# Output products of the second PSUM bank declared independent of the copy that reads the first bank

## Chip, cores and metric

The kernel runs on one core of one Trainium2 chip. The metric is the device time of one execution in microseconds (us). Ratios are the mean time of one kernel's fast runs over the mean of the other's of the same rounds, so they are not quite the ratio of the medians that are quoted. The experiments ran on two chips; each had the kernel before in its rounds but not the changed kernel, so the ratios compare them best, and medians of different experiments should be compared only to about 1 us (those of the kernel before lie between 386.71 and 387.66). Engines: PE is TensorE, PEld its weight loads, DVE VectorE, ACT ScalarE, POOL GpSimd, SP the queue that issues most transfers.

## The reference

```python
w = softmax(weight, axis=-1)                      # 8 heads, 7 taps
x_pad = concat(zeros(B, 6, D), x)                 # B=8, S=4224, D=192
out = einsum('hk,bskhg->bshg', w, windows(x_pad)) # causal conv, one filter per head
proj = out @ w_in                                 # 192 -> 2*512
val, gate = proj[..., :512], proj[..., 512:]
h = a * h + val[:, t]                             # a = exp(A_log)[0], step by step; ys[t] = h
return (silu(gate) * ys) @ w_out                  # 512 -> 192
```

## The kernel before

Tokens are cut into blocks of 960, and the 512 inner channels into four groups of 128; a step is one block with one group. The loop does two steps in each repeat. PE makes value and gate products, each in a "full" part over 128 of the 192 input channels and a "half" part over the other 64; DVE scans the values, ACT takes SiLU of the gates, POOL multiplies. When 512 tokens are ready in all groups, an output unit multiplies them by `w_out`. In PSUM lie two value tiles and two "m" tiles of two banks each; the m tiles serve gates, conv products and output units in turn. ACT copies the conv result to SBUF (tile `yc`), and a DMA transpose turns it into `xc`, which the value and gate products of a later repeat read. Halo rows are the rows ahead of a sequence, which the convolution has to read as zeros.

```python
def out_mm(ps, u, k, cs):                  # bank k of the tile: 2 x 192 columns
    for c in cs:
        for j in range(k * UB // 2, (k + 1) * UB // 2):
            o = k * BANK + (j % 2) * D
            nc.tensor.matmul(ps[:, o : o + D], yr[c][:, ...], wout[:, c, :], ...)

def out_unit(u):
    ps = mtile()
    osb = o_pool.tile([P, UB, D], FP32, name="osb")
    for k in range(2):
        out_mm(ps, u, k, range(NC))        # eight products
        out_copy(nc.scalar, ps, osb, k)    # PSUM bank k -> SBUF, 128x384
    nc.sync.dma_start(o4[u], osb)
# ... in each repeat (s = 2 * p):
scan(s); val(s+1) full; gate(s) full; val(s+1) half; gate(s) half
val(s+2) half; gate(s+1) half; silu(s); mul(s); gate(s+1) full; val(s+2) full; silu(s+1)
scan(s+1); mul(s+1); [big input load]; out_unit(u); [zero halo rows]; conv_piece(...)
```

The framework places the waits. It takes the second eight products as writers of the tile that the first copy is still reading, and makes them wait, though they write another bank.

Of the kernel before, what the change touches and what calls it, by code (L numbers as in the profile page):

```python
# [36 lines left out]
def kernel(  # L37
# [9 lines left out]
    nc = tc.nc  # L47

    B, S, D = x.shape
# [4 lines left out]
    P = 128  # L54
    NC = DI // P
# [22 lines left out]
    of = out.rearrange("b s d -> (b s) d")  # L78
# [14 lines left out]
    def vtile():  # L93
        return ps_v.tile([P, 2 * BANK], FP32, name="pv")

    def mtile():
        return ps_m.tile([P, 2 * BANK], FP32, name="pm")

    def copy(eng, o, i):
        if eng is nc.scalar:  # L100
            eng.copy(o, i)  # L101
        else:
            eng.tensor_copy(o, i)

    def half(b):
        return SIZES[b] * M // 2
# [96 lines left out]
    for r in range(2):  # L203
# [4 lines left out]
        )  # L208
    xt0, _ = xtile(0)
    copy(nc.scalar, xt0[:, n0 : 2 * n0, :], xr[1])  # L210
    copy(nc.vector, xt0[:, 0:n0, :], xr[0])

    pt = mtile()
# [51 lines left out]
    def conv_evac(engs, ps, b, part):  # L265
        n = SIZES[b]
        nh = n // 2
        y = ytile(b)
        E = 2 * G
        pr = ps[0:M, :]  # L270
        W1 = P - 2 * E
        for eng, js in engs:
            j0, nj = js
            if part == 0:
                copy(
                    eng, view(y, j0 * E, [[E, nj], [P, n], [1, E]]),
                    view(pr, j0 * BANK, [[BANK, nj], [E, n], [1, E]]),
                )
            else:
                q = W1 // 2  # L280
                copy(
                    eng, view(y, 2 * E + j0 * q, [[q, nj], [P, n], [1, q]]),
                    view(pr, j0 * BANK, [[BANK, nj], [E, n], [1, q]]),
                )
                z = E - q
                for j in range(j0, j0 + nj):
                    copy(
                        eng,
                        view(y, n * P + j * z, [[P // 2, 2], [P, nh], [1, z]]),
                        view(pr, j * BANK + q, [[nh * E, 2], [E, nh], [1, z]]),  # L290
                    )
# [31 lines left out]
    wout = singles.tile([P, NC, D], BF16, name="wout")  # L323
# [10 lines left out]
    for part in range(2):  # L334
        ps = vtile()
# [64 lines left out]
    yr = [singles.tile([P, RING], BF16, name=f"y_{c}") for c in range(NC)]  # L400

    def ring(t, n):
        r = (t - SHIFT) % RING
        assert r + n <= RING
        return slice(r, r + n)
# [5 lines left out]

    def out_mm(ps, u, k, cs):
        r = ring(u * UT, UT)
        for c in cs:
            for j in range(k * UB // 2, (k + 1) * UB // 2):
                o = k * BANK + (j % 2) * D
                nc.tensor.matmul(  # L417
                    ps[:, o : o + D], yr[c][:, r.start + j * P : r.start + j * P + P],
                    wout[:, c, :], start=(c == 0 and j % 2 == 0), stop=(c == NC - 1),
                    skip_group_check=True,  # L420
                )

    def out_copy(eng, ps, osb, k):
        copy(
            eng, osb[:, k * UB // 2 : (k + 1) * UB // 2, :].rearrange("p b d -> p (b d)"),
            ps[:, k * BANK : k * BANK + 2 * D],
        )

    def out_unit(u):
        ps = mtile()  # L430
        osb = o_pool.tile([P, UB, D], FP32, name="osb")
        for k in range(2):
            out_mm(ps, u, k, range(NC))
            out_copy(nc.scalar, ps, osb, k)
        nc.sync.dma_start(o4[u], osb)

    def conv_piece(b, part):
# [14 lines left out]
    u = 0  # L452
    todo = [(b, part) for b in range(1, NSB) for part in range(2)]
    for p in range(NSTEP // 2):
# [32 lines left out]
        if u < NU - 1 and done_step(u) < s - late:  # L487
            out_unit(u)
            u += 1
# [10 lines left out]
    ps = mtile()  # L500
    for k in range(2):
        out_mm(ps, u, k, range(NC - 1))
    scan(s)
    mul(nc.vector, s)
    osb = o_pool.tile([P, UB, D], FP32, name="osb")
    for k in range(2):
        out_mm(ps, u, k, [NC - 1])
    for k in range(2):
        out_copy((nc.scalar, nc.vector)[k], ps, osb, k)
        h2 = slice(k * UB // 2, (k + 1) * UB // 2)  # L510
        (nc.scalar, nc.sync)[k].dma_start(o4[u, :, h2, :], osb[:, h2, :])
# [28 lines left out]
```

## Time and profile before

| | before |
|---|---|
| time, median | 387.66 us (387.17 to 388.15) |
| span of the profiled run | 385.9 us |
| PE / DVE / POOL / ACT busy | 86 / 80 / 78 / 70% |
| granted PE clock | 0.996 |

The busy shares alone name no culprit: four engines between 70 and 86%. The page's part 4, the chain that ended last by line, does:

```profile
PE pm L417 25%; PE pm L352 15%; PE pv L352 14%; PE pv L358 9%; ACT osb L101 8%; PE pm L248 7%; PE pm L358 7%; DVE h L392 2%; PE pm L187 2%; ACT sg L378 1%; POOL y L410 1%; DMA xc<-yc 1%; ACT yc L101 1%; ACT xb L130 0%; ACT xc L101 0%
```

The path is PE nearly throughout, with one foreign body: ACT's output copy (L101, tile `osb`) has 8% of the span. Since ACT is idle for 30% of the span, this entry points to an order that is enforced, not to a full engine.

### The profile page before, as it was taken

What the parts mean: (1) busy time and instruction counts of PE and PEld (TensorE: products, weight loads), DVE (VectorE), ACT (ScalarE), POOL (GpSimd) and SP (SyncE); (2) the same over time, 40 slices, a digit from 0 to 9 for tenths busy, and PEclk for the clock granted to TensorE, in tenths of its full rate; (3) what the DMA queues carried; (4) which work ended last, traced back from release to release, by engine and by line L of the source; (5) the groups of instructions that cost most, each with busy time, mean ns of one, the idle gap of its engine ahead of it and who ended that gap; (6) DMA issues with size and microseconds to landing.
All of it is one profiled execution on the core that took longest, in us unless ns stands there. A gap on an engine that the chain in (4) does not pass through costs nothing.

```text
span 385.9 us, 6702 instructions
## 1 busy us (share of the span) xinstructions
PE 330.5 (86%) x2555; PEld 194.6 (50%) x2555; DVE 310.2 (80%) x181; ACT 270.2 (70%) x437; POOL 302.7 (78%) x176
## 2 busy tenths in 40 slices
PE   8888888888998888888888888989888888988884
PEld 3444455544554555544555555545555555554553
DVE  3677888879887888878888888898888878888982
ACT  4487677776776777776777677777777777776662
POOL 5867987788778877788789777897789767778891
PEclk9899999999999999999999999999999999999999
DMA  9899999479945996489746994499449954444323
GB/s 186 93 136 132 133 178 208 120 127 189 184 120 122 138 206 155 121 118 177 169 109 123 185 202 121 121 161 219 120 106 153 203 131 111 109 111 112 98 88 125
DMA packets 124523, 55.16 MB, mean 143 GB/s; under 512 B 89622, under 2 KB 124298, under 8 KB 124490
## 3 DMA queue, kind: packets, MB, share of 16 engines
q1 hardware_dynamic: 84498, 39.20, 45.1%
q0 software_dynamic: 39248, 14.99, 34.4%
q10 hardware_dynamic: 744, 0.54, 0.5%
q8 instruction: 20, 0.33, 0.4%
q14 instruction: 13, 0.11, 0.1%
HBM read 31.45 MB, written 25.95 MB: 149 GB/s over the span
## 4 chain that ended last, share of the span: by engine, by line
PE 79%; ACT 11%; issue 4%; DVE 3%; POOL 1%; DMA 1%; DVEq 0%; ACTq 0%
PE pm L417 25%; PE pm L352 15%; PE pv L352 14%; PE pv L358 9%; ACT osb L101 8%; PE pm L248 7%; PE pm L358 7%; DVE h L392 2%; PE pm L187 2%; ACT sg L378 1%; POOL y L410 1%; DMA xc<-yc 1%; ACT yc L101 1%; ACT xb L130 0%; ACT xc L101 0%
## 5 line engine op out<-in xcount | busy, mean ns | idle before, releaser
L410 POOL TENSOR_TENSOR y<-sg,h 128x960 bf16<-128x960 bf16 (+2 forms) x143 | 278.2, 1967 | 71.4 <-ACT sg L378 71.3
L392 DVE TENSOR_TENSOR_SCAN h<-av,h,pv 128x960 bf16<-128x960 f32 (+4 forms) x132 | 261.6, 2018 | 55.8 <-issue 36.8
L378 ACT ACTIVATE sg<-pm 128x960 bf16<-128x960 f32 (+2 forms) x144 | 133.3, 952 | 36.0 <-PE pm L358 30.6
L417 PE MATMUL pm<-wout,y 128*128 128x192 bf16 x1056 | 108.2, 245 | 37.2 <-ACT osb L101 36.8
L417 PEld LDWEIGHTS <-y 128*128 128x128 bf16 x1056 | 89.8, 97 | 60.5 <-issue 47.4
L101 ACT COPY osb<-pm 128x384 f32<-128x384 f32 x131 | 62.6, 478 | 63.0 <-PE pm L417 60.8
L352 PE MATMUL pm<-xc,w 128*128 128x480 bf16 (+2 forms) x288 | 81.9, 366 | 1.1 <-ACT yc L101 0.7
L352 PE MATMUL pv<-xc,w 128*128 128x480 bf16 (+2 forms) x288 | 81.1, 362 | 1.5 <-DVE h L392 1.3
L352 PEld LDWEIGHTS <-w 128*128 128x128 bf16 x576 | 50.0, 98 | 61.6 <-issue 32.5
L101 ACT CAST yc<-pm 96x320 bf16<-96x320 f32 (+2 forms) x140 | 69.6, 552 | 5.1 <-PE pm L248 4.3
L358 PE MATMUL pv<-xc,w 64*128 64x480 bf16 (+2 forms) x288 | 53.1, 366 | 2.4 <-DVE h L392 2.4
L358 PE MATMUL pm<-xc,w 64*128 64x480 bf16 (+2 forms) x288 | 52.4, 361 | 0.0
L392 DVE TENSOR_TENSOR_SCAN h<-av,pv 128x768 bf16<-128x768 f32 (+4 forms) x32 | 45.6, 1434 | 5.2 <-issue 3.5
L358 PEld LDWEIGHTS <-w 64*128 64x128 bf16 x576 | 22.6, 94 | 47.4 <-issue 32.9
L248 PE MATMUL pm<-xb,tb 112*96 112x240 bf16 (+1 forms) x280 | 39.4, 263 | 5.6 <-ACT xb L130 5.3
L248 PEld LDWEIGHTS <-tb 112*96 112x96 bf16 x288 | 30.0, 123 | 8.3 <-issue 6.8
L124 POOL DMA_DIRECT2D xb<-in_x_dram x12 | 17.7, 1473 | 0.1
L187 PE MATMUL pm<-wm 128*128 128x512 bf16 x24 | 8.6, 524 | 1.3 <-DVE wm L141 1.3
L187 PEld LDWEIGHTS <-wm 128*128 128x128 bf16 x24 | 2.9, 128 | 5.6 <-issue 3.8
L101 ACT COPY xc<-pm 128x480 bf16<-128x480 bf16 (+1 forms) x5 | 2.5, 526 | 1.8 <-PE pm L315 1.8
L326 POOL CAST w<-w1r 128x512 bf16<-128x512 f32 x2 | 1.2, 610 | 3.1 <-DMA w1r<-in_moe_w_in_dram 3.0
L315 PE MATMUL pm<-ident,yc 96*128 96x96 bf16 x27 | 1.8, 205 | 2.1 <-ACT xc L101 1.5
(45 smaller groups left out, 23.6 us busy)
## 6 DMA issues: line engine op xcount, KB each, us to landing
out_dram<-osb SPq DMA_DIRECT2D x65, 384.0 KB, 2.8
xb<-in_x_dram POOLq DMA_DIRECT2D x6, 1680.0 KB, 19.3
xb<-in_x_dram POOLq DMA_DIRECT2D x2, 840.0 KB, 9.4
xb<-in_x_dram POOLq DMA_DIRECT2D x1, 1428.0 KB, 15.9
xb<-in_x_dram POOLq DMA_DIRECT2D x3, 420.0 KB, 6.7
xc<-yc SPq DMA_TRANSPOSE x34, 4.8
w1r<-in_moe_w_in_dram SPq DMA_DIRECT2D x1, 448.0 KB, 5.6
xr<-in_x_dram ACTq DMA_DIRECT2D x1, 336.0 KB, 3.7
```

The source lines that it names most:

```text
L101: eng.copy(o, i)
L124: nc.gpsimd.dma_start(xt[:, a0 : a0 + n, :], rows(FIRST[b0], n))
L187: nc.tensor.matmul(pw[:, 0:BANK], wm[:, 0:P], wm, start=True, stop=True)
L248: nc.tensor.matmul(pc[:, :, i * G : i * G + G], tb[:, h, 0:M], xt[:, a0 : a0 + n, h * G : h * G + G], start=True, stop=True, skip_group_ch ...
L315: nc.tensor.transpose(pts[r // 2][:, o + i * M : o + i * M + M], y[:, (r * nh + i) * P : (r * nh + i + 1) * P], ident,)
L326: nc.gpsimd.tensor_copy(w1[:, lo : lo + DI], w1r[:, lo : lo + DI])
L352: nc.tensor.matmul(o, w1[:, m], xc[:, k * w : k * w + w], start=start, stop=not start, skip_group_check=True,)
L358: nc.tensor.matmul(o, w2[r, m], xc[r, 2 * w : 3 * w], start=start, stop=not start, skip_group_check=True,)
L378: nc.scalar.activation(sg[:, 0 : 2 * w], pgs.pop(s)[:, BANK - w : BANK + w], Act.Silu)
L392: nc.vector.tensor_tensor_scan(h[:, lo:hi], av[:, c : c + 1].to_broadcast([P, hi - lo]), pv[:, BANK - w + lo : BANK - w + hi], initial=0.0 ...
L410: eng.tensor_mul(yr[c][:, ring(FIRST[b] * M, n)], sgs.pop(s)[:, 0:n], hs.pop(s)[:, 0:n])
L417: nc.tensor.matmul(ps[:, o : o + D], yr[c][:, r.start + j * P : r.start + j * P + P], wout[:, c, :], start=(c == 0 and j % 2 == 0), stop=( ...
```

## The change

The intent is to let PE write the second bank while ACT reads the first. The instructions and their order stay; only the dependency goes.

```diff
     def out_unit(u):
         ps = mtile()
         osb = o_pool.tile([P, UB, D], FP32, name="osb")
+        first = None
         for k in range(2):
-            out_mm(ps, u, k, range(NC))
-            out_copy(nc.scalar, ps, osb, k)
+            mms = out_mm(ps, u, k, range(NC))
+            if first is not None:
+                apart(mms, first)
+            first = out_copy(nc.scalar, ps, osb, k)
         nc.sync.dma_start(o4[u], osb)
+    def apart(insts, other):
+        for i in insts:
+            tc.declare_no_dep(i.ins, other.ins, reason="another PSUM bank of the same tile")
# cut: copy(), out_mm() and out_copy() now return the instructions they make
```

More of the change, by code (lines that the diff above doesn't have):

```diff
@@ L99, in copy @@
     def copy(eng, o, i):
-        if eng is nc.scalar:
-            eng.copy(o, i)
-        else:
-            eng.tensor_copy(o, i)
+        return eng.copy(o, i) if eng is nc.scalar else eng.tensor_copy(o, i)
     def half(b):
@@ L413, in out_mm @@
         r = ring(u * UT, UT)
+        mms = []
         for c in cs:
@@ L416, in out_mm @@
                 o = k * BANK + (j % 2) * D
-                nc.tensor.matmul(
-                    ps[:, o : o + D], yr[c][:, r.start + j * P : r.start + j * P + P],
-                    wout[:, c, :], start=(c == 0 and j % 2 == 0), stop=(c == NC - 1),
-                    skip_group_check=True,
+                mms.append(
+                    nc.tensor.matmul(
+                        ps[:, o : o + D], yr[c][:, r.start + j * P : r.start + j * P + P],
+                        wout[:, c, :], start=(c == 0 and j % 2 == 0), stop=(c == NC - 1),
+                        skip_group_check=True,
+                    )
                 )
+        return mms
     def out_copy(eng, ps, osb, k):
-        copy(
+        return copy(
             eng, osb[:, k * UB // 2 : (k + 1) * UB // 2, :].rearrange("p b d -> p (b d)"),
```

## The prediction

> **What bounds the kernel now.** I read the page's table of groups and the list of waits first, then the chain of work that ended last, then the timeline of one repeat of the main loop. The groups and waits say how much TensorE (PE) waits for what:
>
> ```profile
> L417 PE MATMUL pm<-wout,y 128*128 128x192 bf16 x1056 | 108.2, 245 | 37.2 <-ACT osb L101 36.8
> PE pm L417 <- ACT osb L101: 36.8, 65, 0.6
> ACT osb L101 <- PE pm L417: 60.8, 68, 0.9
> PE pm L248 <- ACT xb L130: 5.3, 7, 0.9
> ```
>
> The output products (L417) sit idle 36.8 us in 65 waits, every one for an output copy on ScalarE (ACT). Nothing else holds PE for more than 5.3 us. The number 65 is one wait in each output unit of the loop. The chain that ended last shows that the wait is on the path, over and over:
>
> ```profile
> 151.98 0.67 PE pm L417 x8
> 152.66 0.02 issue
> 152.68 0.49 ACT osb L101
> 153.17 0.04 issue
> 153.21 0.82 PE pm L417 x8
> 154.03 0.41 PE pm L248 x4
> ```
>
> Eight products of the first bank, the copy of that bank, then eight products of the second bank: serial, where only the first pair has to be. The engine's timeline of one repeat gives the true size of the hole:
>
> ```profile
> 201.36 0.38 PE L358 MATMUL pv<-xc,w 64*128 64x480 bf16 x2
> 202.69 0.57 PE L352 MATMUL pv<-xc,w 128*128 128x480 bf16 x2
> 203.09 0.82 PE L417 MATMUL pm<-wout,y 128*128 128x192 bf16 x8
> 204.48 0.82 PE L417 MATMUL pm<-wout,y 128*128 128x192 bf16 x8 [0.57 <-ACT osb L101]
> 205.14 0.58 PE L248 MATMUL pm<-xb,tb 112*96 112x240 bf16 x4
> ```
>
> From the start of the second eight to the start of the conv products is 205.14 - 204.48 = 0.66 us: eight products issue in that time when nothing stops them. From the start of the first eight to the second is 204.48 - 203.09 = 1.39 us. So the hole is 1.39 - 0.66 = 0.73 us, more than the 0.57 us printed as idle, because the printed idle starts only when the last product has drained. A repeat (two scan steps) takes 5.10 us: the second eight start at 153.21 and 158.31 in the chain.
>
> What stands next in line is VectorE (DVE) with its scans and GpSimd (POOL) with its multiplies:
>
> ```profile
> 253.76 8.53 DVE L392 TENSOR_TENSOR_SCAN h<-av,h,pv 128x960 bf16<-128x960 f32 x4 [0.74 <-issue]
> 263.31 4.32 DVE L392 TENSOR_TENSOR_SCAN h<-av,h,pv 128x960 bf16<-128x960 f32 x2 [1.02 <-issue]
> PE 330.5 (86%) x2555; PEld 194.6 (50%) x2555; DVE 310.2 (80%) x181; ACT 270.2 (70%) x437; POOL 302.7 (78%) x176
> ```
>
> Four scans back to back take 8.53 us and two take 4.32, so a pair costs 4.21 us in a dense stream: DVE cannot repeat faster than that.
>
> **What the Trainium skill says.** "Perfetto Trace Analysis", section Matmuls under Optimizing Tensor Performance: independent groups should rotate through PSUM banks so that the evacuation of one overlaps the products of the next. The kernel has the two banks but, by the chain above, not the overlap. "PSUM — Partial Sum Buffer", section on bank collisions: two engines in the same bank and quadrant at once is an error, different banks are clean. The two halves lie 512 fp32 apart, a whole bank, so the freed overlap is legal; no run yet shows it. "Perfetto Trace Analysis", section Tensor Engine Instruction: matmul ends in a profile are estimated; that fits the 0.57 printed against 0.73 in start times. "DMA: Bandwidth & Descriptors", section Queues, rings and completion order: each DMA engine goes round between queues a packet at a time, so a big load slows other transfers. The trace agrees: the transposes land in 3.7 to 13.0 us, and the long ones are those beside an input load.
>
> **The change part by part.** No instruction is added, removed or moved; the order on each engine stands. I compared the waits in the two built programs: in the main loop the first product of the second bank loses its wait on ACT. The wait of the copies on their products, of the conv on the SiLU that frees its tile, and of the next gate products on the second copy stay. The return values in the helpers are host-side only.
>
> PE alone would repeat in 5.10 - 0.73 = 4.37 us. I then placed everything from the start of the value half-products that release the second scan (201.36 in the timeline; call it 0):
> - DVE/PE coupling. There are two value tiles. The scan that starts at 0.43 releases the next at 0.43 + 2.11; that one ends and lets PE refill its tile 2.27 after its own start (chain: scan starts 171.87, PE goes 174.14). PE wants that tile at 0.41 + 4.37 = 4.78, and gets it at 2.54 + 2.27 = 4.81. That 0.03 is spread over two repeats: about 4.385 us each.
> - ACT. First copy 2.58 to 3.06 (after both SiLUs, 0.62 to 2.50), second 3.24 to 3.72, conv evacuation 3.70 to 4.77. The gate products that need the second copy come at 3.86, so there is 0.1 us of slack; ACT work sums to 1.88 + 2 x 0.48 + 1.07 = 3.9 us.
> - POOL: 4 multiplies take 7.87 us in a dense stretch, 3.93 a repeat, 5.7 in the few with a DMA issue (1.8). Its products are read at least two steps later, so it should not bind.
>
> Sum: about 55 repeats with conv and output unit gain 5.10 - 4.385 = 0.715 each, 39.3 us. Some 6 at the end have no conv (4.69 us now, at 360.57 and 365.26 on DVE); there the gate products come 0.41 earlier and wait about 0.3 for the second copy, so the repeat becomes about 4.27: 6 x 0.42 = 2.5. The first four units lie in the start, which waits for loads: perhaps 1.5 together. The four repeats without an output unit (4.43 us now, bound by DVE) give 0.5. Together 43.8 us: 387.7 - 43.8 = 343.9 us if nothing new waits.
>
> **The rivals.**
> 1. DMA turns into a new wait. A block's transpose is issued in one repeat and its result is first read exactly three repeats later by the program's order: 15.3 us now, 3 x 4.385 = 13.1 us after. Six or seven transposes are issued some 5 us after a 1680 KB load and land only when that load is nearly through:
>
> ```profile
> xb<-in_x_dram POOLq DMA_DIRECT2D x6, 1680.0 KB, 19.3
> xc<-yc SPq DMA_TRANSPOSE x34, 4.8
> DMA to landing us min/median/max: 3.7/4.8/13.0
> DMA to landing us min/median/max: 11.7/11.7/11.7
> DMA to landing us min/median/max: 12.5/12.5/12.5
> ```
>
> (The last three lines are all transposes, then those issued at 89.00 and 211.95.) Stores and transposes now come 16% more densely beside the load, and POOL issues the load later against PE, so I expect these landings at 13 to 15 us: a stall of 0 to 2 us on about 7 occasions. I charge 7 x 0.7 = 5 us; at the worst it is 14. For it speaks that the margin was only 2.3 us; against it, that DMA moved 208 GB/s in one slice and averages 143.
> 2. DVE becomes the bound with more loss than I count. At 4.21 of 4.385 us it has 4% left; if each scan gap cost 0.1 more, 65 x 0.2 = 13 us would be lost: 357.
> 3. The wait moves: ACT's copies become late and hold the gate or conv tile. If the whole first copy returned this way, the time would be near 388 and nothing gained; the 0.1 us slack makes a partial return possible, not a whole one, since ACT has over 0.4 us free a repeat.
> 4. Only the printed idle returns: 36.8 us, 351.
>
> **Range and chances.** 343.9 + 5 = 348.9, rounded to 348.5 us. With no DMA stall and a little more at the start, 341; with a DMA stall near its worst or rival 2 in part, 357. Faster by over 2% needs under 380: nearly all the expected gain would have to vanish. Chances: faster 0.97, same 0.025, slower 0.005.
>
> **What would show it.** Right: no waits of L417 on ACT (up to a few us left); repeats of 4.37 to 4.45 us between conv starts; DVE near 90% busy; PE waiting for DVE in short pieces of under 0.1 us; the first eight and second eight in one run of sixteen. Rival 1: PE or its weight loads waiting for the transposed tile about seven times, at load times, with landings above 13 us. Rival 2: repeats over 4.5 us without DMA waits, PE waiting for scans. Rival 3: gate or conv products waiting for the output copy. I would be wrong if the second bank's products still wait for the first copy, or if the granted clock (0.996) falls with the denser PE.

## The result, and the profile after

The changed kernel takes 345.56 us (344.59 to 346.46, 4 runs) against 387.42 in the same rounds: a ratio of 0.8917 (95% interval 0.8887 to 0.8948). Executions over 1.5% slower than the fastest of the same kernel are left out of the means. Lines have moved by one or three: L416 is the output product, L100 the copy, L389 the scan, L355 the half products, L245 the conv. From the page, parts 1 and 5:

```profile
PE 321.2 (93%) x2555; PEld 193.7 (56%) x2555; DVE 309.9 (90%) x181; ACT 272.0 (79%) x437; POOL 302.8 (88%) x176
L416 PE MATMUL pm<-wout,y 128*128 128x192 bf16 x1056 | 97.9, 246 | 0.8 <-POOL y L407 0.6
```

DVE, ACT and POOL work as long as before (309.9 against 310.2 us on DVE) in a shorter span, so every share rose. The idle time of the output products fell from 37.2 us to 0.8, and ACT is no longer among its causes. PE's "busy" fell by 9 us though it does the same products: the products start every 0.08 us and each is printed with 0.25 us, so that two runs of eight are printed with 2 x 0.82 = 1.64 us and one of sixteen with 1.48.

PE's timeline of one repeat after:

```profile
97.37 1.48 PE L416 MATMUL pm<-wout,y 128*128 128x192 bf16 x16
98.69 0.57 PE L245 MATMUL pm<-xb,tb 112*96 112x240 bf16 x4
99.51 0.57 PE L349 MATMUL pm<-xc,w 128*128 128x480 bf16 x2
101.74 1.48 PE L416 MATMUL pm<-wout,y 128*128 128x192 bf16 x16
```

and ACT's of the same stretch:

```profile
98.23 0.48 ACT L100 COPY osb<-pm 128x384 f32<-128x384 f32 x1
98.89 0.48 ACT L100 COPY osb<-pm 128x384 f32<-128x384 f32 x1 [0.18 <-PE pm L416]
```

The two eights are one run of sixteen: from its start to the conv products 98.69 - 97.37 = 1.32 us, where before it was 205.14 - 203.09 = 2.05. The first copy starts at 98.23, inside the run, on the bank that PE has left. The second copy ends at 99.37 and the gate products that reuse its tile start at 99.51. From unit to unit 4.37 us (101.74 - 97.37).

What PE waits for now (list of waits: total us, times, longest):

```profile
PEld L355 <- DMA xc<-yc: 5.7, 5, 2.4
PE pm L245 <- ACT xb L127: 5.3, 7, 0.9
PE pv L355 <- DMA xc<-yc: 3.4, 4, 2.0
PE pv L355 <- DVE h L389: 2.8, 5, 0.7
PE pv L349 <- DVE h L389: 1.2, 3, 0.4
```

The first and third lines are the same waits, seen at the weight loads and at the products: a transposed block that has not landed. Before there was one such wait of 0.7 us. One of them, in the timeline of PE and then in the chain of work:

```profile
169.63 0.38 PE L355 MATMUL pv<-xc,w 64*128 64x480 bf16 x2 [0.56 <-DMA xc<-yc]
```

```profile
155.69 13.90 DMA xc<-yc
169.59 0.05 issue
169.63 0.38 PE pv L355 x2
```

The transpose was issued at 155.69, 4.4 us behind a 1680 KB load (151.27), and took 13.90 us.

To find where the time went I took the starts of all value products that open a repeat from both traces and set the repeats side by side, in program order:

| repeats | before, us each | after, us each | gain |
|---|---|---|---|
| first 6 (start-up) | 5.34 | 5.23 | 0.6 us |
| 44 ordinary | 5.10 | 4.415 (24 take 4.38, the others 4.42 to 4.54) | 30.2 us |
| 3 ordinary with a late transpose | 5.10 | 4.87, 5.06, 5.12 | 0.3 us |
| 5 with halo zeroing | 6.00 | 5.28 | 3.6 us |
| 8 irregular (no output unit, beside one, short block) | | | 3.6 us |
| 5 without conv, at the end | 4.47 | 4.03 | 2.2 us |

The sum is 40.5 us; the ramps ahead of and behind these repeats give 1.2 more, which makes the 41.7 us between the spans. The ordinary repeats that are longer than 4.38 us lose the time at the half value products of the step after next, which write the tile that the scan has just read. Two such places in PE's timeline:

```profile
118.63 0.36 PE L355 MATMUL pm<-xc,w 64*128 64x480 bf16 x2
118.88 0.38 PE L355 MATMUL pv<-xc,w 64*128 64x480 bf16 x2
```

```profile
123.07 0.37 PE L355 MATMUL pm<-xc,w 64*128 64x480 bf16 x2
123.27 0.36 PE L355 MATMUL pv<-xc,w 64*128 64x480 bf16 x2
```

In the second the value products follow at 0.20 us, the usual spacing. In the first they follow at 0.25 us, and a scan had ended at 118.83, 0.05 us before them. So it is in 19 of the 20 longer repeats: the value products are 0.03 to 0.15 us late and start 0.05 us after a scan's end. The 20th has a short wait for a transpose. In the 24 repeats of 4.38 us the scan had ended 0.06 us or more before.

### The profile page after: what moved, and what is told of

Read it like the earlier page. It is cut to its first block, busy times and chain, and to the rows that moved or that the text cites. A ratio compares the mean times of both kernels' runs of the same rounds, so it can differ in the third digit from the quotient of the medians.

```text
span 344.2 us, 6702 instructions
## 1 busy us (share of the span) xinstructions
PE 321.2 (93%) x2555; PEld 193.7 (56%) x2555; DVE 309.9 (90%) x181; ACT 272.0 (79%) x437; POOL 302.8 (88%) x176
## 4 chain that ended last, share of the span: by engine, by line
PE 47%; DMA 4%; ACT 1%; issue 1%; POOL 1%; DVE 0%; DVEq 0%; ACTq 0%
PE pm L416 15%; PE pm L349 10%; PE pv L349 8%; PE pv L355 6%; DMA xc<-yc 4%; PE pm L355 4%; PE pm L245 4%; POOL y L407 1%; ACT sg L375 0%; ACT osb L100 0%; DVE h L389 0%; ACT xb L127 0%; DVE osb L100 0%; DVEq L389 0%; ACTq L375 0%
## 5 line engine op out<-in xcount | busy, mean ns | idle before, releaser
L389 DVE TENSOR_TENSOR_SCAN h<-av,h,pv 128x960 bf16<-128x960 f32 (+4 forms) x132 | 261.5, 2018 | 19.2 <-POOL y L407 5.6
L375 ACT ACTIVATE sg<-pm 128x960 bf16<-128x960 f32 (+2 forms) x144 | 135.1, 953 | 39.9 <-PE pm L355 30.5
L416 PE MATMUL pm<-wout,y 128*128 128x192 bf16 x1056 | 97.9, 246 | 0.8 <-POOL y L407 0.6
L416 PEld LDWEIGHTS <-y 128*128 128x128 bf16 x1056 | 89.0, 98 | 14.6 <-POOL y L407 0.8
L100 ACT COPY osb<-pm 128x384 f32<-128x384 f32 x131 | 62.8, 479 | 16.3 <-PE pm L416 14.1
L100 ACT CAST yc<-pm 96x320 bf16<-96x320 f32 (+2 forms) x140 | 69.6, 552 | 5.0 <-PE pm L245 4.3
L355 PE MATMUL pv<-xc,w 64*128 64x480 bf16 (+2 forms) x288 | 53.2, 364 | 6.4 <-DMA xc<-yc 3.4
L355 PEld LDWEIGHTS <-w 64*128 64x128 bf16 x576 | 23.0, 94 | 53.5 <-issue 37.1
L355 PE MATMUL pm<-xc,w 64*128 64x480 bf16 (+2 forms) x288 | 52.4, 358 | 0.0
L389 DVE TENSOR_TENSOR_SCAN h<-av,pv 128x768 bf16<-128x768 f32 (+4 forms) x32 | 45.5, 1432 | 1.6 <-PE pv L355 1.0
L245 PE MATMUL pm<-xb,tb 112*96 112x240 bf16 (+1 forms) x280 | 39.4, 263 | 5.7 <-ACT xb L127 5.3
L245 PEld LDWEIGHTS <-tb 112*96 112x96 bf16 x288 | 29.9, 123 | 8.3 <-issue 7.0
L100 ACT COPY xc<-pm 128x480 bf16<-128x480 bf16 (+1 forms) x5 | 2.5, 527 | 1.8 <-PE pm L312 1.8
```

Source lines behind the costliest of these rows:

```text
L100: return eng.copy(o, i) if eng is nc.scalar else eng.tensor_copy(o, i)
L245: nc.tensor.matmul(pc[:, :, i * G : i * G + G], tb[:, h, 0:M], xt[:, a0 : a0 + n, h * G : h * G + G], start=True, stop=True, skip_group_ch ...
L355: nc.tensor.matmul(o, w2[r, m], xc[r, 2 * w : 3 * w], start=start, stop=not start, skip_group_check=True,)
L375: nc.scalar.activation(sg[:, 0 : 2 * w], pgs.pop(s)[:, BANK - w : BANK + w], Act.Silu)
L389: nc.vector.tensor_tensor_scan(h[:, lo:hi], av[:, c : c + 1].to_broadcast([P, hi - lo]), pv[:, BANK - w + lo : BANK - w + hi], initial=0.0 ...
L416: nc.tensor.matmul(ps[:, o : o + D], yr[c][:, r.start + j * P : r.start + j * P + P], wout[:, c, :], start=(c == 0 and j % 2 == 0), stop=( ...
```

## The experiments

**1. Half of the units.** If each removed wait is worth its hole between starts (0.73 us) and not the printed idle (0.57 us), half of the declarations tell the two apart.

```diff
-            if first is not None:
+            if first is not None and u % 2 == 0:
                 apart(mms, first)
```

> The changed kernel with the second bank's products declared independent only in output units of even number (33 of the 65 units in the loop). Theory (each removed wait is a hole of 0.73 us between starts): half of the stall of 47.5 us returns, about 33 x 0.73 = 24 us, with little given back because the average repeat stays above VectorE's pace: 387.4 - 24 = 363 to 364 us. Rival (only the printed idle of 0.57 us returns in each unit, and the rest of the gain came from elsewhere): 387.4 - 33 x 0.57 = 368.6 us. Printed waits of the output products on the copy: 32, 0.57 us each.

Measured: 365.02 us (364.92 to 367.17), ratio 0.9447 (0.9416 to 0.9478). The list of waits:

```profile
PE pm L416 <- ACT osb L100: 18.1, 32, 0.6
```

32 waits are left of 65, so 33 went. From the starts, the holes of the remaining units sum to 23.5 us of 47.6 before, so 24.1 us or 0.73 each went; the time fell by 21.7 us, 0.66 for each. The time alone does not tell the two values apart: 0.66 is halfway between 0.73 and 0.57. The starts do, for the holes that went were of 0.73 us. The time is 1 us beyond the upper end of what I expected, and the starts show where the difference lies: 2.7 us more of waiting had gathered at the half value products, the place where scans and transposes are awaited.

**2. The products together, the copies behind them, nothing declared.** This takes away the wait in the middle without overlapping copy and products.

```diff
         for k in range(2):
             out_mm(ps, u, k, range(NC))
+        for k in range(2):
             out_copy(nc.scalar, ps, osb, k)
```

> The kernel before, with all sixteen output products ahead of both copies in the program and nothing declared, so that no copy stands between the products, but both copies start only after the sixteenth. Theory (it is the overlap of the first copy with the second eight products that pays, because the next gate products need the second copy and have 0.1 us of slack): the second copy ends about 0.48 us later than in the changed kernel, gate products wait about 0.38 us for the output copy, a repeat is 4.7 to 4.8 us, in all 365 to 370 us. Rival (only the removal of TensorE's wait in the middle counts): the same as the changed kernel, 345 to 347 us.

Measured: 359.42 us (358.15 to 359.96), ratio 0.9284 (0.926 to 0.9309). Both expectations missed: it is far from the changed kernel's time, as the theory says, but almost 6 us under its range. PE's timeline and the list of waits:

```profile
106.36 0.57 PE L352 MATMUL pv<-xc,w 128*128 128x480 bf16 x2
107.06 0.57 PE L352 MATMUL pm<-xc,w 128*128 128x480 bf16 x2
```

```profile
PE pm L352 <- ACT osb L101: 0.7, 2, 0.4
```

The gate products start 0.70 us after the value products where 0.41 is the usual spacing: a hole of 0.29 us, not the 0.38 I had put, because the two copies now run back to back and take 0.86 us together, not twice 0.48. "ScalarE: Activation LUTs", section What ACT_TABLE_LOAD costs, says that back-to-back ACTIVATEs overlap by about 93 ns; here the copies overlap by 2 x 0.478 - 0.86 = 0.10. An ordinary repeat is 4.67 us. The list of waits shows only 2 of these holes: of the 0.29 us, 0.16 lies under the printed end of the products before (106.36 + 0.57 = 106.93), and the 0.13 us of idle that is left is too short for the list, whose shortest entries here have 0.2 us. So the order alone brings two thirds of the gain, 27 us, and the overlap of copy and products the rest.

**3. The first copy done twice.** Is ACT free to be slower, at 79% busy?

```diff
-            if first is not None:
-                apart(mms, first)
-            first = out_copy(nc.scalar, ps, osb, k)
+            for c in first or []:
+                apart(mms, c)
+            first = [out_copy(nc.scalar, ps, osb, k) for _ in range(2 - k)]
```

> The changed kernel with the first bank's copy done twice in each unit of the loop (same data, 0.48 us more on ScalarE), both declared apart from the second bank's products. Theory (ScalarE has about 0.1 us of slack in its chain: the second copy releases the gate products): the second copy ends about 0.3 us later, gate products wait about 0.2 us for the output copy, 345.5 + 65 x 0.2 = 358 us, 353 to 362. Rival (a copy off the products' path is free, ScalarE is only 79% busy): within 2 us of 345.5.

Measured: 351.09 us (350.85 to 351.63), ratio 0.9066 (0.9034 to 0.9097). So 5.5 us slower than the changed kernel: not free, but less than half of the 12.5 us I expected, and 2 us below my range. In the starts the excess at the gate products (what their spacing has above the usual 0.41 us) rises by 7.7 us, from 2.2 to 9.9, and an ordinary repeat is 4.52 us, 0.11 more than 4.41 and not 0.2 more: the wait of 0.14 us at the gates takes the place of the 0.03 us that PE lost to DVE on average. ACT's slack in the chain is real and about 0.1 us.

**4. and 5. One useless memset on VectorE in each repeat,** in the changed kernel and in the one before.

```diff
+        nc.vector.memset(wm, 0.0)
         if p < NSTEP // 2 - 1:
             scan(s + 1)
```

> The changed kernel with a memset of 128x256 words (0.27 us, useless) on VectorE between the two scans of each repeat. Theory (after the change VectorE and TensorE are level, 4.21 against 4.37 us a repeat, the slack is gone): the pair of scans becomes about 4.5 us and sets the repeat, 4.5 to 4.6 us instead of 4.41, in all 351 to 356 us. Rival (TensorE alone binds and VectorE still has room): within 1 us of 345.5.

> The kernel before with the same useless memset on VectorE in each repeat. Theory (before the change VectorE had 0.8 us of room in each repeat of 5.10 us): at most 2 us slower, 387 to 389.5 us, the difference from the few repeats without an output unit and from the end. Rival (VectorE's work adds directly): 72 x 0.27 = 19 us slower, 407 us.

Measured: 345.19 us (ratio 0.8925, 0.8896 to 0.8953) for the changed kernel with it, 386.92 us (ratio 1.0, 0.9977 to 1.0022) for the kernel before with it. The first expectation missed: nothing was lost. DVE's timeline, with the memset and then of the changed kernel without it:

```profile
104.15 0.27 DVE L487 MEMSET wm<- 128x256 uint32 x1
104.34 2.14 DVE L389 TENSOR_TENSOR_SCAN h<-av,pv 128x960 bf16<-128x960 f32 x1
```

```profile
104.86 2.15 DVE L389 TENSOR_TENSOR_SCAN h<-av,pv 128x960 bf16<-128x960 f32 x1 [0.18 <-issue]
```

The memset holds the next scan for 0.19 us, not 0.27, and stands where DVE was idle for 0.18 us anyway, waiting for the half products. The dose was as large as the room, so the run could not decide.

**6. and 7. Two memsets,** the second of which waits for the first (0.58 us from the first memset's start to the scan, 97.15 to 97.73).

> The changed kernel with two useless memsets between the two scans of a repeat. In the run with one, the memset fell into a gap that VectorE had: the second scan waits for TensorE's half-products anyway, and 0.21 us more on VectorE just filled the difference between 4.21 and 4.41 us. Theory (VectorE's room is only about 0.2 us a repeat): the second memset, which waits for the first, adds 0.25 to 0.3 us to every repeat, 62 to 65 repeats, 16 to 19 us: 358 to 366 us. Rival (VectorE has room of 0.5 us or more): within 3 us of 345.5.

> The kernel before with the same two memsets. Theory (0.8 us of room in each repeat of 5.10 us): 387 to 390 us. Rival: 16 us or more slower, as in the changed kernel.

Measured: 363.65 us (ratio 0.9407, 0.9383 to 0.943) and 386.64 us (ratio 0.9997, 0.998 to 1.0014). PE's waits in the changed kernel with two, then in the kernel before with two:

```profile
PE pv L355 <- DVE h L389: 16.8, 56, 0.7
```

```profile
PE pv L358 <- DVE h L392: 2.7, 5, 0.7
```

The same 0.58 us cost the changed kernel 18 us and the kernel before nothing. So DVE had room for all of it before and has room for about 0.2 us a repeat now. The change used up DVE's slack: in an ordinary repeat a still faster PE would soon wait for the scans.

**8. The big loads one repeat earlier.** Are the late transposes a matter of phase?

```diff
-        if s % NC == 0 and b % XG == 2 and b + 6 < NSB:
-            load_cast(b + 6, min(b + 6 + XG, NSB))
+        if s % NC == 2 and b % XG == 1 and b + 7 < NSB:
+            load_cast(b + 7, min(b + 7 + XG, NSB))
```

> The changed kernel with the big input loads issued one repeat earlier, so that no transpose is issued just behind a load. Theory (a part of what was given back are transposes that land after 13 us, beside a load): TensorE's waits for the transposed tile after the start (0.32, 0.51, 0.56 us and a short one) go to nearly 0 and the time falls by 1 to 2 us against 345.5. Rival (the transposes are slow from the total traffic whatever the phase): the waits stay or move to the next transposes, time within 0.5 us of 345.5.

Measured: 343.55 us (342.58 to 345.33, 6 runs), ratio 0.8873 (0.8843 to 0.8902).

```profile
PE pv L355 <- DMA xc<-yc: 2.1, 1, 2.1
```

The one wait left lies in the start-up (32.19 us). All later ones are gone, as expected. The transposes did not become fast: in this trace those of the steady loop that are issued 8 to 9 us behind a load still took 9.2 to 12.9 us, against 12.9 to 14.0 when issued close behind one. They now fit into their three repeats of about 4.4 us, 13.2 us together. The time is 2 us lower by medians, but the two intervals overlap: the waits are shown, their worth in time by this run alone is not.

**9. and 10. Halo rows zeroed ahead of the output copies,** in the changed kernel and in the one before.

```diff
+        if b >= 2 and todo and todo[0][1] == 0:
+            zero_halos(todo[0][0])
         late = 0 if b >= NSB - 5 else 2
         if u < NU - 1 and done_step(u) < s - late:
             out_unit(u)
# in the conv loop, where it stood, it is left for b < 2 only
```

> The changed kernel with the zeroing of the halo rows (0.28 us on ScalarE, 7 times) put ahead of the output unit's copies instead of behind them, so that the conv products do not wait 0.74 us for it. Theory (the largest wait of TensorE that is left sits on the path): each of the 6 in the steady loop falls from 5.28 to about 4.4 us, 5 us in all, 340 to 341.5 us. Rival (VectorE, level with TensorE, takes the place of the wait): under 2 us gained, 344 us.

> The kernel before with the same earlier zeroing of halo rows. Theory: VectorE has room here, so the gain is the full 6 x 0.9 = 5.4 us: 381.5 to 382.5 us. Rival: none of it on the path, 387 us.

Measured: 341.81 us (339.87 to 343.26, the 5 fast runs of 6; ratio 0.8822, 0.8788 to 0.8856) and 382.86 us (ratio 0.9874, 0.983 to 0.9918). The time fell by 3.7 and 4.4 us by medians, a little less than expected in both (a fraction of 1 us outside either range). In the starts the excess at the conv products fell from 7.7 to 3.2 us, 4.5 us, in both: the loop has five such repeats and not six, each worth 0.9. In the changed kernel the waits for transposes after the start were longer in this trace, 0.48, 1.04 and 1.44 us against 0.32, 0.51 and 0.56, which fits the part that is missing.

**11. Both edits together.**

> The changed kernel with both edits together: halo rows zeroed ahead of the output copies, and the big loads issued one repeat earlier. Theory (two separate waits on TensorE's path): 3.7 us of the first and at least 1.7 of the second, more because the earlier zeroing alone raised the waits for transposes (0.48, 1.04, 1.44 us): 338.5 to 340.5 us, and no wait for the transposed tile after the start. Rival (VectorE or GpSimd takes the place): 341.5 us or more, with TensorE waiting for scans instead.

Measured: 338.5 us (337.51 to 338.55, 4 runs), ratio 0.8749 (0.8733 to 0.8765).

```profile
PE pm L245 <- ACT xb L127: 1.6, 2, 0.9
PE pv L355 <- DMA xc<-yc: 1.0, 1, 1.0
PE pv L355 <- DVE h L389: 3.0, 6, 0.7
```

The halo waits fall from 5.3 to 1.6 us, and the one wait for a transpose is in the start-up. Waits for scans hardly grew (3.0 us against 2.8). The five repeats with halo zeroing went from 5.28 to 4.38 or 4.44 us. This is the fastest version found, 7 us under the changed kernel. Its interval lies below that of the earlier zeroing alone (0.8788 to 0.8856), which shows that the shifted loads are worth time; by medians 3 us on top of the zeroing.

## Why the prediction was right

The time, 345.56 us, lies in the range of 341 to 357 and 3 us under the point. By its steps:

- *The hole is 0.73 us, not 0.57.* Shown: the run of sixteen is 0.73 us shorter, the 65 holes sum to 47.6 us in the starts before and 0.1 after, and half of the declarations take away 24.1 us of them.
- *DVE/PE coupling makes the repeat 4.385 us.* 4.415 measured over the 44 undisturbed repeats, mostly in turns of 4.38 and 4.44. The size was off by 0.03. That DVE is the partner is shown by the two memsets and by the starts: 19 of the 20 longer repeats resume 0.05 us after a scan's end. The alternation vanishes where a repeat is 4.52 or 4.67 us. The short waits for DVE that I announced do not show as printed idle, only in the starts.
- *ACT has 0.1 us of slack.* The second copy ends 0.14 us ahead of the gates' start; the doubled copy took that away and cost 5.5 us. Rival 3 did not happen in the changed kernel, and the second experiment shows what it would have cost.
- *The DMA becomes a new wait: 7 x 0.7 = 5 us.* The mechanism is shown: transposes behind a load took 12.9 to 14.0 us against 11.3 to 13.0 before, and moving the loads removed the waits. The term was mis-sized: three steady repeats lost 0.46, 0.65 and 0.70 us, 1.8 us in all, and not seven. The other landings fitted into their three repeats. I had charged every occasion; the overcharge (5 charged, 1.8 found) is as large as the 3 us between point and result. Without the charge I had written 343.9, and the kernel with shifted loads, which has no such waits after the start, ran at 343.55. That the agreement is so close is in part luck, because the misses of the other terms, below and in the table, cancel: 43.8 us were forecast without the charge, and 41.7 + 1.8 = 43.5 us found.
- *Start +1.5, repeats without output unit +0.5, end +2.5.* Measured 0.6, nothing (two take 3.65 us in PE's starts before and after, two about 4.1), and 2.2. Against this stand 1.2 us in the ramps and 57 repeats with conv and output unit where I counted 55. The start had a wait for a transpose of 1.97 us that I had not foreseen.
- *The granted clock and the shares.* The clock stayed at 0.992 to 1.0 in the runs of the changed kernel, and DVE is 90% busy, as announced.
- *Rivals 2 and 4.* Neither holds. DVE is close to binding but costs only the 0.03 us; and more than the printed idle returned, though the 36.8 us of rival 4 lay only 5 us from the result, so that the total alone could hardly have told them apart. The starts do.

## What to carry to other kernels

Measure a wait between instruction starts, undisturbed against disturbed, since printed idle on PE leaves out what the modelled drain covers. Before taking a wait away, lay out one repeat with the engines next in line and count how many repeats each transfer has to land; here VectorE came within 0.2 us of the new pace and the transposes overran it. When two accesses share a tile and not a bank, say so to the scheduler: reordering alone brought two thirds of the gain.

## What the Trainium skill lacked or had wrong

- "Perfetto Trace Analysis", section Tensor Engine Instruction, says that the ends of matmuls are estimated, but not that this hides a part of real waits: holes of 0.73 us between starts are printed as 0.57, and with the copies behind all products a hole of 0.29 us leaves 0.13 us of printed idle.
- "DMA: Bandwidth & Descriptors", section Queues, rings and completion order, gives the round by packets but no size for the effect. In the changed kernel's loop a transpose that lands in 3.7 to 5.5 us when issued 21 us or more behind a load took 12.9 to 14.0 us when issued 3.6 to 4.4 us behind a 1680 KB load.
- "PSUM — Partial Sum Buffer", section on bank collisions, holds: ACT read one bank during PE's writes to the next in 65 units, with a correct result in each experiment built on the change. It lacks that a framework may track tiles and not banks, which cost 42 us here.
